# One attention unit for the 64-token tiles of two batches: one in each half of the 128 rows

## The chip, the cores and the metric

The kernel runs on one core of one Trainium2 chip. The metric is the device time of one execution, in microseconds (us). Times of instructions come from one profiled execution of the kernel.

## What is computed

Sliding-window attention with a linear bias by distance, then two feed-forward layers without a norm between them. Everything is float32.

```
B, H, S, D = 4, 8, 576, 64          # attention, window 128
scores = q @ k.T / 8 + slope[h] * -(i - j)      where 0 <= i - j < 128, else masked
attn   = softmax(scores);  x = attn @ v         -> 2304 tokens x 512
h = x @ w_in;   x = (h * sigmoid(h)) @ w_out     # 512 -> 2048 -> 512
h = relu(x @ w_in2);  out = (h * h) @ w_out2     # 512 -> 2048 -> 512
```

A batch has 576 tokens: four tiles of 128 and a last one of 64. Two heads make a pair; q and k come transposed, with the 64 numbers of the one head of a pair in rows 0 to 63 and those of the other in rows 64 to 127.

## The kernel before

**Blocks and units.** The 16 full tiles of the four batches make four blocks of 512 tokens, the four tiles of 64 tokens a fifth one of 256. A *unit* is one tile and one pair of heads: 64 full units (0 to 63), then 16 narrow ones (64 to 79), each of which fills rows 0 to 63 alone in the work by row.

**What is done for a unit.** `scores` (L247): TensorE, one matmul for each half of the query rows and each head, into one of two PSUM tiles, `so` (the first two of four units) or `pp` (the other two). `maxima` (L273, VectorE): bias and row minimum. `exponentials` (L283, ScalarE), `reciprocals` (L290, VectorE), `normalise` (L300, GpSimd). `transpose_p` (L331, TensorE, again into `so` and `pp`), `copy_p` (L344, or L347 and L348 for narrow units, ScalarE), `values` or, for narrow units, `values_of_four` (L380, L361, TensorE, into `o`), `x_hi` (L391, ScalarE) and `x_lo` (L395, VectorE): the block's x as the sum of two reduced floats.

**Slots.** From unit 20 on attention runs inside the loop of the first layer. A *slot* n (0 to 63, L1019) is one chunk of 128 columns of w_in for one block of 512 tokens: 12 matmuls of 128x512 in `mm1` (L564). All engines get their instructions in the order in which this loop writes them. Four units go together: scores of units u to u+3 in slot n = u - 20 ahead of its `mm1`; transposes in slot n+3; values in slot n+7 (n+6 where they are narrow):

```
for n in range(4, (NB - 1) * NF, 4):
    u = n0 + n
    narrow = u < NU and units[u][4] < P
    visits[n][2] = some(*range(u, u + 4))
    visits[n + 2 if narrow else n + 3][0] = some(*range(u - 4, u))
    visits[n + 3][1] = some(*range(u, u + 4))
```

Here [2] are scores, [1] transposes, [0] values. At the end of a slot come the loads: q and k of units u+4 to u+7 in the slot of the scores of u to u+3, v of the next four units in the slot of the values of four. Tiles "q", "k" and "v" have four buffers each. The last line of a slot is `store_t(n - 2)`.

**Queues.** Nearly all DMAs are issued by SyncE (SP), in order: an issue that waits holds all that stand behind it. `act1(n)` (L582, ScalarE) writes tanh(h/2) of slot n to one of four buffers, `ts[:, n % 4]`; `store_t(n)` (L592) sends it to DRAM (`g0d`), and `act1(n + 4)` waits for that store to land. ScalarE's order in a slot with values and transposes is `act1(n - 1)`, `x_hi`, `copy_p`; the next scores into `so` and `pp` wait for the copies out of them.

**Weights.** w_in and w_out are brought in as 64-bit words and converted, one tile of two chunks at a time, in five steps in slots that follow each other (`w_first`, `w_abs`, `w_join`, `w_hi`, `w_lo`); `begin` (L841) says in which slot a tile begins. The 16 buffers "w" hold the 16 converted tiles in the end; until then some serve as `spare` room.

After slot 63 come slots of the fifth block (L553), the second matmul (L631), and the second layer (L692, L785).

Of the kernel before, what the change touches and what calls it, by code (L numbers as in the profile page):

```python
# [8 lines left out]
F32 = mybir.dt.float32  # L9
# [7 lines left out]
P = 128  # L17
# [8 lines left out]
def kernel(  # L26
# [21 lines left out]
    nc = tc.nc  # L48
    B, NHP, S, _ = v.shape
    NT, DM = out.shape  # L50
    NF = w1.shape[0]
    D = 64
# [18 lines left out]
    full = [(b, t, P, min(t, P)) for b in range(B) for t in range(0, S - P + 1, P)]  # L71
    rest = [(b, S // P * P, S % P, P) for b in range(B)]
    blocks = [full[i:i + NSUB] for i in range(0, len(full), NSUB)]
    blocks.append(rest)
    NB = len(blocks)
    width = [sum(t[2] for t in tiles) for tiles in blocks]
    start = [sum(width[:j]) for j in range(NB)]
    assert sum(width) == NT and max(width) <= BLK and P % rest[0][2] == 0
    tbs = []
    for j, tiles in enumerate(blocks):  # L80
        c0 = 0
        for t in tiles:
            tbs.append((j, c0) + t)
            c0 += t[2]
    units = [t + (hp,) for t in tbs for hp in range(NHP)]
    NU = len(units)
    x_t = {}

# [6 lines left out]
    def attention(ap, ps, n0):  # L95
        slope = [2.0 ** (-8.0 * (h + 1) / H) for h in range(H)]
        xq, xk, xv, z_t, s_t, pt_t, o_t = ({} for _ in range(7))
        c = {"n0": n0}

        W = 3 * D

        def halves_of(u):

            n, m0 = units[u][4:6]
            if m0 == P:
                return [(slice(0, n), slice(0, W))]
            if u < c["n0"] and not m0:
                return [(slice(0, n), slice(D, W))]  # L110
            return [(slice(i * D, (i + 1) * D), slice(P - m0 - i * D, W)) for i in range(n // D)]

        def whole(u):

            n, m0 = units[u][4:6]
            return slice(0, n), slice(D + P - m0 - (n - D if m0 < P else 0), D + W)

        def zeros(z):
            nc.gpsimd.memset(z[..., :D], 0.0)
            nc.gpsimd.memset(z[..., D + W:], 0.0)  # L120

# [70 lines left out]
        def load_v_strip(i):  # L192
# [6 lines left out]
            for hp in range(NHP):  # L199
                xv[i * NHP + hp] = [c["va"][:, i - 1, hp] if m0 else None, c["va"][:, i, hp]]  # L200

        def load_qk(u):
            _, _, b, t0, n, m0, hp = units[u]
            if u not in xq:
                xq[u] = ap.tile([P, P], F32, tag="q", name="q", bufs=4)
                nc.sync.dma_start(out=xq[u][:, :n], in_=q[b, hp, :, t0:t0 + n])
            xk[u] = ap.tile([P, 2 * P], F32, tag="k", name="k", bufs=4)[:, P - m0:P + n]
            nc.sync.dma_start(out=xk[u], in_=k[b, hp, :, t0 - m0:t0 + n])

        def load_v(u):  # L210
            _, _, b, t0, n, m0, hp = units[u]
            t = ap.tile([P, 2, P], F32, tag="v", name="v", bufs=4)
            if m0 == n:
                nc.sync.dma_start(
                    out=t, in_=v[b, hp, t0 - m0:t0 + n, :].rearrange("(k p) d -> p k d", p=P)
                )
            else:
                if m0:
                    nc.sync.dma_start(out=t[:m0, 0], in_=v[b, hp, t0 - m0:t0, :])
                nc.sync.dma_start(out=t[:n, 1], in_=v[b, hp, t0:t0 + n, :])  # L220
            xv[u] = [t[:, 0], t[:, 1]]

        def scores(u):


            _, _, b, t0, n, m0, hp = units[u]
            lo = P - m0
            xq_, xk_ = xq.pop(u), xk.pop(u)
            apart = len(xq_.shape) == 3
            if apart:  # L230
                s = acc_p.tile([P, 2, 2 * P], F32, tag="acc", name="s")
                s = [s[:, j] for j in range(2)]
            else:
                so = c["pp" if u >= c["n0"] and u % 4 > 1 else "so"]
                s = [so[:, j, u % 2 * 2 * P:(u % 2 + 1) * 2 * P] for j in range(2)]
            if u < c["n0"] and not m0:
                for j in range(2):
                    nc.tensor.matmul(
                        s[j][:D, D:P], lhsT=c["far"], rhs=c["ident"][:, :D], start=True, stop=True
                    )  # L240
            for i in range(n // D):
                for j in range(2):
                    r = slice(i * D, (i + 1) * D)
                    first = max(lo - i * D, 0)
                    keys = slice(first + i * D - lo, W + i * D - lo)
                    h = slice(0, P) if apart else slice(j * D, (j + 1) * D)
                    nc.tensor.matmul(  # L247
                        s[j][r, first:W], lhsT=xq_[:, j, r] if apart else xq_[h, r], rhs=xk_[h, keys],
                        start=True, stop=True,
                    )  # L250
            s_t[u] = s
# [96 lines left out]
                copy(to[:n, :, 1::2], pp[:n, :, 1::2])  # L348
            pt_t[u] = pt

        def values_of_four(u):

            *_, n, m0, _ = units[u]
            pts, vts = [[t.pop(u + i) for i in range(4)] for t in (pt_t, xv)]
            o = c["o"]
            for i in range(4):
                o_t[u + i] = o[:, i - i % 2:i - i % 2 + 2]
            for kb, m in ((0, m0), (1, n)):
                for i in range(4):
                    for j in range(2):  # L360
                        nc.tensor.matmul(  # L361
                            o[j * D:(j + 1) * D, i, :n], lhsT=vts[i][kb][:m, j * D:(j + 1) * D],
                            rhs=pts[i][:m, j, kb, :n], start=kb == i == 0, stop=kb == 1,
                            skip_group_check=True,
                        )

        def values(u):
            _, _, b, t0, n, m0, hp = units[u]
            pt, vt = pt_t.pop(u), xv.pop(u)
            if u % 2 == 0:  # L370
                o = c["o"]
                if u < c["n0"] - 4 and u % 4:
                    o = c.pop("late", None) or acc_p.tile([P, 4, P], F32, tag="acc", name="o")
                first = u % 4 if u >= c["n0"] - 4 else 0
                o_t[u] = o[:, first:first + 2]
            o = o_t[u - u % 2][:, u % 2]
            for kb, m in ((0, m0), (1, n)):
                if m:
                    for j in range(2):
                        nc.tensor.matmul(  # L380
                            o[j * D:(j + 1) * D, :n], lhsT=vt[kb][:m, j * D:(j + 1) * D],
                            rhs=pt[:m, j, kb, :n], start=kb == 0 or not m0, stop=kb == 1,
                        )
# [9 lines left out]
        def x_lo(u):  # L393
            xh, xl, o = halves_of_x(u)
            nc.vector.tensor_tensor(xl, o, xh.bitcast(F32), ALU.subtract)  # L395

        return (zeros, lambda: c["z"], wake, constants, biases, load_q_apart, load_k_strip, load_v_strip, load_qk, load_v, scores, maxima, exponentials,
                reciprocals, normalise, transpose_p, copy_p, values, values_of_four, x_hi, x_lo)

# [2 lines left out]
    def spare(dtype):  # L404

        return wp.tile([P, 16 * P], F32R, tag="w", name="spare").bitcast(dtype)
# [123 lines left out]
    for b in range(NB):  # L530
        m = BLK // width[b]
        slots += [(b, tuple(range(f, f + m))) for f in range(0, NF, m)]
    NS = len(slots)
    NI = NF // 2
# [304 lines left out]
    begin = {}  # L839
    for i in range(NI):  # L840
        begin[0, 0, i] = 2 * i - 4  # L841
        begin[0, 1, i] = 2 * NI + 5 * i
    converted = [(0, 0, i) for i in range(EARLY + 1)]
    begin[0, 0, EARLY + 1] = 1

# [35 lines left out]
    with tc.manual_schedule():  # L881
        def ends(j):

            return sum(1 for u in units if u[0] <= j)

        n0 = ends(0) + 4
        with tc.tile_pool(name="at", bufs=2) as ap, tc.tile_pool(
            name="ps", bufs=1, space=bass.MemoryType.PSUM
        ) as ps:
            (zeros, at_z, wake, constants, biases, load_q_apart, load_k_strip, load_v_strip, load_qk, load_v, scores, maxima, exponentials,  # L890
             reciprocals, normalise, transpose_p, copy_p, values, values_of_four, x_hi, x_lo) = attention(ap, ps, n0)
            assert [t[1:4] for t in blocks[0]] == [(i * P, P, min(i, 1) * P) for i in range(NSUB)]
            load_k_strip(0, slice(0, 1))
            load_q_apart(0)
# [100 lines left out]
            def some(*us):  # L995
                return [u for u in us if u < NU]
# [4 lines left out]
            visits = {n: [(), (), ()] for n in range((NB - 1) * NF)}  # L1001
            for n in range(4, (NB - 1) * NF, 4):
                u = n0 + n
                narrow = u < NU and units[u][4] < P
                visits[n][2] = some(*range(u, u + 4))
                visits[n + 2 if narrow else n + 3][0] = some(*range(u - 4, u))
                visits[n + 3][1] = some(*range(u, u + 4))
            u = n0
            visits[1] = (), (u - 2, u - 1), ()
# [8 lines left out]
            left = []  # L1018
            for n in range((NB - 1) * NF):  # L1019
                old, mid, new = visits[n]  # L1020
                if len(old) == 4 and units[old[0]][4] < P:
                    values_of_four(old[0])
                else:
                    for u in old:
                        values(u)
                for u in mid:
                    transpose_p(u)
                for u in new:
# [51 lines left out]
        with tc.tile_pool(name="gp", bufs=1) as gp_, tc.tile_pool(  # L1080
            name="acc2", bufs=4, space=bass.MemoryType.PSUM
# [29 lines left out]
            for i in range(4):  # L1111
                n = 4 + 10 * i
# [9 lines left out]
            for j, x in enumerate(((1, 1, 3), (1, 1, 4))):  # L1122
                n = 18 + 10 * j
# [5 lines left out]
            for i in range(5, NI):  # L1129
                n = (29, 42, 57)[i - 5]  # L1130
# [23 lines left out]
            for s in range(1, 4):  # L1154
                c = 7 * 4 * s - 21
# [57 lines left out]
            for n in range(NS):  # L1213
# [6 lines left out]
                b, fs = slots[n]  # L1220
# [22 lines left out]
            for c in range(4 * NI // 2):  # L1243
                s = 2 * c // NI
# [105 lines left out]
```

## Time and profile before

| | us |
|---|---|
| runs of the kernel, median (lowest to highest) | 871.03 (869.74 to 871.57) |
| the profiled execution, its time | 870.38 |
| its span in the trace | 868.6 |
| TensorE busy in the span | 857.1 |
| slots 44 to 63, from the first scores of a narrow unit to the end of slot 63 | 209.38 to 283.83 of the span |

In the rows, PE is TensorE's matmuls and PEld its weight loads, DVE is VectorE, ACT ScalarE, POOL GpSimd, SPq the issues of SyncE. A float32 matmul of the program is two records of the trace, so 8 matmuls of attention are 16 records; those of `mm1` are one each.

### The profile page before, as it was taken

The page shows a single profiled execution, that of the slowest core. Times are in us where ns is not written, and L with a number is a line of the kernel's source. Part 1 is how long each engine was busy: PE and PEld are TensorE (multiplying, and loading weights), DVE is VectorE, ACT ScalarE, POOL GpSimd, SP SyncE. Part 2 cuts the span into 40 slices and gives each one's busy share as a digit, 9 for nine tenths or more (in the row PEclk, how much of TensorE's full clock was granted, in tenths as well). Part 3 has the DMA queues.
Part 4 walks back from the last instruction along what each step waited for, and adds up shares of the span by engine and source line. Part 5 has one row for each costly group of instructions (what it writes and reads, how often), then busy time and mean ns, then how long its engine had stood idle before and what let it go on. Part 6 is the DMA issues. An engine that isn't in the chain of part 4 may idle for free.

```text
span 868.6 us, 17368 instructions
## 1 busy us (share of the span) xinstructions
PE 857.1 (99%) x6344; PEld 763.4 (88%) x6344; DVE 595.2 (69%) x1290; ACT 460.5 (53%) x1010; POOL 137.1 (16%) x222
## 2 busy tenths in 40 slices
PE   7999999999999999999999999999999999999997
PEld 6778888787778888888888899999999999999997
DVE  6878665656552465998646546677467799989883
ACT  8778666666563443555333456556566743343331
POOL 6788333434431000000000000000000000000000
PEclk9999999999999999999999999999999999999999
DMA  9676766776542377799875454565457954444431
GB/s 265 196 220 220 209 187 188 216 224 193 153 147 97 117 256 248 261 345 355 278 275 193 145 179 160 197 248 194 160 201 300 348 178 148 135 147 129 138 108 39
DMA packets 114469, 173.64 MB, mean 200 GB/s; under 512 B 12240, under 2 KB 73680, under 8 KB 111824
## 3 DMA queue, kind: packets, MB, share of 16 engines
q1 hardware_dynamic: 114112, 172.40, 60.2%
q8 instruction: 50, 0.82, 0.4%
q14 instruction: 35, 0.29, 0.1%
q10 hardware_dynamic: 272, 0.13, 0.1%
HBM read 111.15 MB, written 61.34 MB: 199 GB/s over the span
## 4 chain that ended last, share of the span: by engine, by line
PE 94%; DMA 2%; SPq 1%; DVE 1%; ACT 1%; POOL 1%; issue 0%; DVEq 0%; ACTq 0%; POOLq 0%
PE acc L631 23%; PE acc L785 21%; PE h L564 19%; PE a L692 12%; PE d L692 6%; PE b L692 3%; PE o L380 3%; PE h L553 3%; PE so L247 1%; PE pp L331 1%; PE pp L247 1%; DMA g0d<-t 1%; PE so L331 1%; DMA spare<-in_w_dram 1%; PE o L361 1%; SPq L174 1%
## 5 line engine op out<-in xcount | busy, mean ns | idle before, releaser
L631 PE MATMUL acc<-g,w 128*128 128x512 f32 (+1 forms) x896 | 196.9, 382 | 0.0
L631 PEld LDWEIGHTS acc<-g,w 128*128 128x128 f32 x896 | 163.8, 188 | 32.9
L564 PE MATMUL h<-x,w 128*128 128x512 f32 x768 | 185.7, 396 | 0.0
L785 PE MATMUL acc<-w,g 128*128 128x256 f32 x1512 | 181.6, 283 | 0.0
L785 PEld LDWEIGHTS acc<-w,g 128*128 128x128 f32 x1512 | 181.5, 192 | 0.0
L564 PEld LDWEIGHTS h<-x,w 128*128 128x128 f32 x768 | 141.2, 188 | 34.6 <-DVE st L273 2.5
L692 PE MATMUL a<-x,w 128*128 128x288 f32 x720 | 104.0, 295 | 0.0
L692 PEld LDWEIGHTS a<-x,w 128*128 128x128 f32 x720 | 98.6, 188 | 0.2 <-DVE ev L823 0.2
L611 ACT CAST g<-l 128x512 fp32r<-128x512 f32 x72 | 44.8, 622 | 99.0 <-PE acc L631 84.8
L612 DVE TENSOR_TENSOR g<-l,g 128x512 fp32r<-128x512 f32 x72 | 49.7, 690 | 54.7 <-ACT g L611 54.3
L300 POOL TENSOR_SCALAR z<-z,st 128x192 f32<-128x192 f32 (+2 forms) x120 | 62.4, 537 | 108.0 <-DVE st L294 77.3
L587 DVE SCALAR_TENSOR_TENSOR t<-t,h 128x512 f32<-128x512 f32 x64 | 43.7, 683 | 47.9 <-ACT t L582 47.8
L582 ACT ACTIVATE t<-h 128x512 f32<-128x512 f32 x64 | 38.2, 596 | 53.3 <-PE h L564 45.4
L283 ACT ACTIVATE z<-z,st 128x192 f32<-128x192 f32 (+2 forms) x120 | 52.3, 438 | 14.8 <-DVE st L273 14.6
L759 ACT CAST g<-l 128x1024 fp32r<-128x1024 f32 x25 | 26.2, 1050 | 61.1 <-issue 30.8
L692 PE MATMUL d<-x,w 128*128 128x288 f32 x384 | 56.4, 295 | 0.0
L692 PEld LDWEIGHTS d<-x,w 128*128 128x128 f32 x384 | 52.9, 188 | 0.0
L273 DVE CUSTOM_DVE_ANT_0 z<-so,bias 128x192 f32<-128x192 f32 (+2 forms) x68 | 19.5, 328 | 30.2 <-PE so L247 26.5
L453 POOL TENSOR_TENSOR w<-spare,w 128x512 fp32r<-128x512 f32 x24 | 36.8, 1553 | 5.7 <-ACT w L448 5.6
L1272 DVE TENSOR_TENSOR ev<-a,ev 128x288 f32<-128x288 f32 x32 | 14.1, 454 | 32.7 <-PE a L692 32.0
L766 DVE TENSOR_TENSOR g<-l,g 128x1024 fp32r<-128x1024 f32 x25 | 30.6, 1224 | 8.2 <-ACT g L759 8.2
L523 DVE TENSOR_TENSOR w<-raw,w 128x1024 fp32r<-128x1024 f32 (+1 forms) x22 | 23.7, 1087 | 10.1 <-ACT w L518 10.1
(160 smaller groups left out, 1157.6 us busy)
## 6 DMA issues: line engine op xcount, KB each, us to landing
g0d<-t SPq DMA_DIRECT2D x72, 256.0 KB, 2.8
l<-g0d SPq DMA_DIRECT2D x72, 256.0 KB, 5.0
raw<-in_w_dram SPq DMA_DIRECT2D x28, 512.0 KB, 5.4
g1d<-t SPq DMA_DIRECT2D x48, 288.0 KB, 2.4
l<-g1d SPq DMA_DIRECT2D x50, 256.0 KB, 3.3
spare<-in_w_dram SPq DMA_DIRECT2D x12, 1024.0 KB, 8.0
wd<-raw SPq DMA_DIRECT2D x10, 1024.0 KB, 4.7
raw<-wd SPq DMA_DIRECT2D x7, 1024.0 KB, 5.7
```

The costliest lines, as they stand in the source:

```text
L283: nc.scalar.activation(z[r, j, k], z[r, j, k], AF.Exp, bias=least[r, j:j + 1], scale=-1.0, accum_out=total[r, j:j + 1],)
L300: nc.gpsimd.tensor_scalar(z[r, j, k], z[r, j, k], share[r, j:j + 1], 1.0, ALU.mult, ALU.mult)
L453: nc.gpsimd.tensor_tensor(w[:, 1, a], words(x)[1][:, a].bitcast(F32), w[:, 0, a].bitcast(F32), ALU.subtract)
L564: nc.tensor.matmul(h[:, j * w:(j + 1) * w], lhsT=wi[:, wh, c * P:(c + 1) * P], rhs=x[:, xh, c, :w], start=c == 0 and i == 0, stop=c == KC ...
L582: nc.scalar.activation(t_t[n], h_t[n], AF.Tanh, scale=0.5)
L587: nc.vector.scalar_tensor_tensor(t, t, 1.0, h, ALU.add, ALU.mult)
L611: nc.scalar.copy(g[:, 0], t)
L612: nc.vector.tensor_tensor(g[:, 1], t, g[:, 0].bitcast(F32), ALU.subtract)
L631: nc.tensor.matmul(to, lhsT=wo[:, a, c * P:(c + 1) * P], rhs=g[:, z, j * w:(j + 1) * w], start=f == 0 and i == 0, stop=f == NF - 1 and i = ...
L692: nc.tensor.matmul(acc[to], lhsT=w[wh][:, c * P:(c + 1) * P], rhs=o[:, xh, c], start=r in (0, 1, 3) and c == 0 and k == 0, stop=c == 1 and ...
L766: tt(g[1][:, :, :4], a, g[0][:, :, :4].bitcast(F32), ALU.subtract)
L785: nc.tensor.matmul(acc[to][:, half], lhsT=g[x][a], rhs=w[y][:, b], start=i == 0 and half == 0 and j == 0, stop=i == NI - 1 and j == 2, ski ...
```

## The change

The fifth block's units are made over: unit 64 to 71 instead of 64 to 79, each with the 64-token tiles of two batches, b and b+1, in rows 0 to 63 and 64 to 127. Such a *double* unit has the shapes of a full one in scores, maxima, exponentials, transposes and copies, and the rules for full units place it: scores in slots 44 and 48, transposes in 47 and 51, values in 51 and 55. For each it loads a q tile from two batches and two k tiles, one for each batch. The second k tile is taken from tag "v", which full units use for v. The v rows of two batches and all four pairs go to one shared tile `c["vs"]` (a "w" buffer, two corners set to zero by GpSimd), by four DMAs for four units. w_out tile 6 begins in slot 53 instead of 46, tile 7 in 56 instead of 51.

```diff
-    units = [t + (hp,) for t in tbs for hp in range(NHP)]
+    units = [t + (hp,) for t in tbs[:len(full)] for hp in range(NHP)]
+    twos = [t[:4] + (P, P) for t in tbs[len(full)::2]]
+    units += [t + (hp,) for t in twos for hp in range(NHP)]
...
+        def load_double_qk(u):
+            _, _, b, t0, _, _, hp = units[u]
+            xq[u] = ap.tile([P, P], F32, tag="q", name="q", bufs=4)
+            nc.sync.dma_start(
+                out=xq[u].rearrange("p (b c) -> p b c", b=2),
+                in_=q[b:b + 2, hp, :, t0:t0 + D].rearrange("b p c -> p b c"),
+            )
+            xk[u] = [
+                ap.tile([P, 2 * P], F32, tag=tag, name=tag, bufs=4)[:, :W] for tag in "kv"
+            ]
+            for i, to in enumerate(xk[u]):
+                nc.sync.dma_start(out=to, in_=k[b + i, hp, :, t0 - P:t0 + D])
+
+        def load_double_v(u):
+
+            _, _, b, t0, _, _, hp = units[u]
+            if hp == 0:
+                if "vs" not in c:
+                    c["vs"] = spare(F32).rearrange("p (h i k d) -> p i k h d", h=NHP, i=2, k=2)
+                    nc.gpsimd.memset(c["vs"][D:, 0, 1], 0.0)
+                    nc.gpsimd.memset(c["vs"][:D, 1, 0], 0.0)
+                for i, kb, r, t in (
+                    (0, 0, slice(0, P), t0 - P), (0, 1, slice(0, D), t0),
+                    (1, 0, slice(D, P), t0 - P), (1, 1, slice(0, P), t0 - D),
+                ):
+                    nc.sync.dma_start(
+                        out=c["vs"][r, i, kb],
+                        in_=v[b + i, :, t:t + r.stop - r.start, :].rearrange("h p d -> p h d"),
+                    )
+            xv[u] = c["vs"][:, :, :, hp]
...
-        def values_of_four(u):
...
+        def values_of_double(u, o):
+            pt, vt = pt_t.pop(u), xv.pop(u)
+            for kb in range(2):
+                for i in range(2):
+                    for j in range(2):
+                        h, r = (slice(x * D, (x + 1) * D) for x in (j, i))
+                        nc.tensor.matmul(
+                            o[h, r], lhsT=vt[:, i, kb, h], rhs=pt[:, j, kb, r],
+                            start=kb == i == 0, stop=kb == 1, skip_group_check=True,
+                        )
...
-        begin[0, 1, i] = 2 * NI + 5 * i
+        begin[0, 1, i] = 2 * NI + 5 * i + (i == 6) * 7 + (i == 7) * 5
...
-                narrow = u < NU and units[u][4] < P
-                visits[n + 2 if narrow else n + 3][0] = some(*range(u - 4, u))
+                visits[n + 3][0] = some(*range(u - 4, u))
```

The order of the instructions on TensorE, first before, from the scores of units 68 to 71 (slot 48) to the transposes of the same units (slot 51; of these 16 rows the first two stand here):

```order
L247 MATMUL so<-k,q 64x192 x4
L247 MATMUL pp<-k,q 64x192 x4
L564 MATMUL h<-x,w 128x512 x24
L361 MATMUL o<-pt,v 64x64 x16
L564 MATMUL h<-x,w 128x512 x12
L331 MATMUL so<-ident,z 128x64
L331 MATMUL so<-ident,z 64x64
```

And of the changed kernel, from the scores' last row in slot 48 to slot 64 (its line 604 is the old line 564, its line 400 is `values_of_double`):

```order
L290 MATMUL pp<-v,q 64x192 x2
L604 MATMUL h<-x,w 128x512 x36
L400 MATMUL o<-pt,spare 64x64 x32
L374 MATMUL so<-ident,z 128x64 x16
L374 MATMUL pp<-ident,z 128x64 x16
L604 MATMUL h<-x,w 128x512 x48
L400 MATMUL o<-pt,spare 64x64 x32
L604 MATMUL h<-x,w 128x512 x108
```

Values and transposes now stand beside each other in one slot, there are two groups of four units instead of four, and nine slots of `mm1` follow without attention.

The second place is SyncE's queue at the end of slot 40, where q and k of units 64 to 67 are loaded; the word "waits" lists what an issue waits for (DMAHW: an earlier DMA, PE: a matmul). Before:

```order
L208 DMA k<-in_k_dram 128x192 [waits DMAHW2_49]
L206 DMA q<-in_q_dram 128x64 [waits DMAHW3_49,PE_49]
L208 DMA k<-in_k_dram 128x192 [waits DMAHW4_49]
L206 DMA q<-in_q_dram 128x64 [waits DMAHW5_49,PE_49]
L208 DMA k<-in_k_dram 128x192 [waits DMAHW6_49]
L206 DMA q<-in_q_dram 128x64 [waits DMAHW7_49,PE_49]
L208 DMA k<-in_k_dram 128x192 [waits DMAHW0_49]
L592 DMA g0d<-t 128x512 [waits DMAHW1_49,DVE_49]
```

In the changed kernel, from the k tile of the first batch of unit 64 to the same store (line 632):

```order
L220 DMA k<-in_k_dram 128x192 [waits DMAHW2_49]
L220 DMA v<-in_k_dram 128x192 [waits DMAHW4_49,DMAHW3_49,PE_49]
L212 DMA q<-in_q_dram 128x2x64
L220 DMA k<-in_k_dram 128x192 [waits DMAHW5_49]
L220 DMA v<-in_k_dram 128x192 [waits DMAHW6_49,PE_49]
L212 DMA q<-in_q_dram 128x2x64 [waits DMAHW7_49]
L220 DMA k<-in_k_dram 128x192 [waits DMAHW0_49]
L220 DMA v<-in_k_dram 128x192 [waits DMAHW1_49,PE_49]
L212 DMA q<-in_q_dram 128x2x64 [waits DMAHW2_49]
L220 DMA k<-in_k_dram 128x192 [waits DMAHW3_49]
L220 DMA v<-in_k_dram 128x192 [waits DMAHW4_49,PE_49]
L632 DMA g0d<-t 128x512 [waits DMAHW5_49,DVE_49]
```

Four loads into tiles "v" have come in. Each takes the buffer of the v tile of a full unit (56 for the first one), and the matmul that it waits for is the last one of that unit's values, in slot 43. The store in the last row is `store_t(38)`. The same order stands at the end of slot 44, for units 68 to 71, the values of units 60 to 63 (slot 47), and `store_t(42)`.

## Rows read from the trace of the kernel before

**Rows 1.** The page, part 1: busy time of the engines.
```profile
PE 857.1 (99%) x6344; PEld 763.4 (88%) x6344; DVE 595.2 (69%) x1290; ACT 460.5 (53%) x1010; POOL 137.1 (16%) x222
```
**Rows 2.** Stretches: us, busy us of five engines (instructions), granted clock, DMA share, GB/s.
```profile
209.38:283.83 74.45, 74.45 (x529) 58.39 (x529) 33.84 (x116) 39.13 (x131) 22.18 (x38) 1.00 0.45 144
...
864.10:868.60 4.50, 0.00 (x0) 0.00 (x0) 1.33 (x3) 0.00 (x0) 0.00 (x0) 1.00 0.31 117
```
**Rows 3.** Timeline of TensorE, four full units: start, us, line, operation, records.
```profile
187.53 1.97 PE L380 MATMUL o<-pt,v 128*64 128x128 f32 x32
189.43 0.71 PE L331 MATMUL so<-ident,z 64*128 64x64 f32 x16
...
190.57 3.01 PE L564 MATMUL h<-x,w 128*128 128x512 f32 x12
193.51 0.88 PE L247 MATMUL so<-k,q 64*64 64x192 f32 x16
194.21 0.83 PE L247 MATMUL pp<-k,q 64*64 64x192 f32 x16
194.97 8.49 PE L564 MATMUL h<-x,w 128*128 128x512 f32 x36
```
**Rows 4.** Timeline of TensorE, narrow units, slots 50 to 54 and 58 to 63.
```profile
232.56 1.30 PE L361 MATMUL o<-pt,v 128*64 128x64 f32 x32
233.79 3.04 PE L564 MATMUL h<-x,w 128*128 128x512 f32 x12
236.76 0.68 PE L331 MATMUL so<-ident,z 64*128 64x64 f32 x8
...
237.84 3.03 PE L564 MATMUL h<-x,w 128*128 128x512 f32 x12
240.80 0.87 PE L247 MATMUL so<-k,q 64*64 64x192 f32 x8
...
242.24 5.78 PE L564 MATMUL h<-x,w 128*128 128x512 f32 x24
247.95 1.30 PE L361 MATMUL o<-pt,v 128*64 128x64 f32 x32
...
268.61 11.19 PE L564 MATMUL h<-x,w 128*128 128x512 f32 x48
279.73 1.30 PE L361 MATMUL o<-pt,v 128*64 128x64 f32 x32
```
**Rows 5.** Timeline of all engines, slots 31 and 32; brackets: idle before, what ended it.
```profile
160.95 0.60 ACT L582 ACTIVATE t<-h 128x512 f32<-128x512 f32 x1 [4.13 <-DMA g0d<-t]
...
161.96 0.68 ACT L348 COPY pt<-so 128x256 f32<-128x256 f32 x2
...
162.69 0.88 PE L247 MATMUL so<-k,q 64*64 64x192 f32 x16
```
**Rows 6.** Timeline of all engines, slot 43.
```profile
204.10 1.92 SPq L214 DMA_DIRECT2D v<-in_v_dram  x4
204.87 0.58 ACT L582 ACTIVATE t<-h 128x512 f32<-128x512 f32 x1
...
206.13 1.08 ACT L344 COPY pt<-so 128x512 f32<-128x512 f32 x2
...
207.09 1.10 ACT L344 COPY pt<-pp 128x512 f32<-128x512 f32 x2
```
**Rows 7.** Timeline, issues of q and k: one in slot 40, first and last of eight in slot 48.
```profile
196.42 1.48 SPq L208 DMA_DIRECT2D k<-in_k_dram  x1
...
225.99 0.33 SPq L206 DMA_DIRECT2D q<-in_q_dram  x1
...
229.24 0.42 SPq L208 DMA_DIRECT2D k<-in_k_dram  x1
```
**Rows 8.** DMA issues in 160 to 217 and 216 to 290: median us to landing.
```profile
g0d<-t SPq DMA_DIRECT2D x15, 256.0 KB, 3.3
...
g0d<-t SPq DMA_DIRECT2D x21, 256.0 KB, 2.2
```

More of the change, by code (lines that the diff above doesn't have):

```diff
@@ L84 @@
             c0 += t[2]
-    units = [t + (hp,) for t in tbs for hp in range(NHP)]
+    units = [t + (hp,) for t in tbs[:len(full)] for hp in range(NHP)]
+    twos = [t[:4] + (P, P) for t in tbs[len(full)::2]]
+    assert rest[0][2] == P // 2 and len(rest) % 2 == 0
+    units += [t + (hp,) for t in twos for hp in range(NHP)]
     NU = len(units)
@@ L102, in attention, with double @@
         W = 3 * D
+        def double(u):
+            return units[u][0] == NB - 1
         def halves_of(u):
@@ L200, in load_v_strip @@
                 xv[i * NHP + hp] = [c["va"][:, i - 1, hp] if m0 else None, c["va"][:, i, hp]]
+        def load_double_qk(u):
[26 more added lines that the diff above has]
+            xv[u] = c["vs"][:, :, :, hp]
         def load_qk(u):
+            if double(u):
+                return load_double_qk(u)
             _, _, b, t0, n, m0, hp = units[u]
@@ L210, in load_v @@
         def load_v(u):
+            if double(u):
+                return load_double_v(u)
             _, _, b, t0, n, m0, hp = units[u]
@@ L229, in scores @@
             apart = len(xq_.shape) == 3
+            if not double(u):
+                xk_ = [xk_[..., max(i * D - lo, 0):W + i * D - lo] for i in range(n // D)]
             if apart:
@@ L244, in scores @@
                     first = max(lo - i * D, 0)
-                    keys = slice(first + i * D - lo, W + i * D - lo)
                     h = slice(0, P) if apart else slice(j * D, (j + 1) * D)
                     nc.tensor.matmul(
-                        s[j][r, first:W], lhsT=xq_[:, j, r] if apart else xq_[h, r], rhs=xk_[h, keys],
+                        s[j][r, first:W], lhsT=xq_[:, j, r] if apart else xq_[h, r], rhs=xk_[i][h],
                         start=True, stop=True,
@@ L349, in copy_p @@
             pt_t[u] = pt
-        def values_of_four(u):
[L353 to L359, printed above, removed]
+        def values_of_double(u, o):
+            pt, vt = pt_t.pop(u), xv.pop(u)
+            for kb in range(2):
+                for i in range(2):
                     for j in range(2):
+                        h, r = (slice(x * D, (x + 1) * D) for x in (j, i))
                         nc.tensor.matmul(
-                            o[j * D:(j + 1) * D, i, :n], lhsT=vts[i][kb][:m, j * D:(j + 1) * D],
-                            rhs=pts[i][:m, j, kb, :n], start=kb == i == 0, stop=kb == 1,
-                            skip_group_check=True,
+                            o[h, r], lhsT=vt[:, i, kb, h], rhs=pt[:, j, kb, r],
+                            start=kb == i == 0, stop=kb == 1, skip_group_check=True,
                         )
@@ L368, in values @@
             _, _, b, t0, n, m0, hp = units[u]
-            pt, vt = pt_t.pop(u), xv.pop(u)
             if u % 2 == 0:
@@ L376, in values @@
             o = o_t[u - u % 2][:, u % 2]
+            if double(u):
+                return values_of_double(u, o)
+            pt, vt = pt_t.pop(u), xv.pop(u)
             for kb, m in ((0, m0), (1, n)):
@@ L397, in attention @@
         return (zeros, lambda: c["z"], wake, constants, biases, load_q_apart, load_k_strip, load_v_strip, load_qk, load_v, scores, maxima, exponentials,
-                reciprocals, normalise, transpose_p, copy_p, values, values_of_four, x_hi, x_lo)
+                reciprocals, normalise, transpose_p, copy_p, values, x_hi, x_lo)
     w_t, raw_t = {}, {}
@@ L890 @@
             (zeros, at_z, wake, constants, biases, load_q_apart, load_k_strip, load_v_strip, load_qk, load_v, scores, maxima, exponentials,
-             reciprocals, normalise, transpose_p, copy_p, values, values_of_four, x_hi, x_lo) = attention(ap, ps, n0)
+             reciprocals, normalise, transpose_p, copy_p, values, x_hi, x_lo) = attention(ap, ps, n0)
             assert [t[1:4] for t in blocks[0]] == [(i * P, P, min(i, 1) * P) for i in range(NSUB)]
@@ L1020 @@
                 old, mid, new = visits[n]
[L1021 to L1025, printed above, removed]
+                for u in old:
+                    values(u)
                 for u in mid:
```

## The prediction

> **What bounds the kernel now.** I read the page's busy times first: TensorE works 857.1 us, 99% of the span, VectorE 69%, ScalarE 53%, GpSimd 16% [rows 1]. A kernel so full gets shorter only by less work on TensorE, and longer by a wait that TensorE has not had. Next the table of stretches. From the first scores of a narrow unit to the end of slot 63, 74.45 us, which holds all that the change touches, TensorE is busy 74.45 of 74.45 us, at a granted clock of 1.00, the upper level (2.4 GHz); ScalarE is busy for 39, VectorE for 34 and GpSimd for 22 us [rows 2]. So the other engines' instructions that vanish there save nothing. What a piece of attention costs is read from TensorE's timeline, once where four full units are worked on [rows 3] and once where four narrow ones are [rows 4]: always from the start of a piece to the start of the next, since the durations in a row overlap. Last come the timelines of all engines and the landing of the stores [rows 5 to 8], for the new waits.
>
> **Less work on TensorE.** Sixteen narrow units are four groups of four; the eight double ones are two, and a double unit has the shapes of a full one.
>
> Scores: a narrow group takes 242.24 - 240.80 = 1.44 us [rows 4], a full one, with twice the records, 194.97 - 193.51 = 1.46 [rows 3]. Four of the one for two of the other: 5.76 to 2.92, a gain of 2.84. The matmuls of the two row halves evidently run beside each other in a full unit. A double unit's k and q also come in the two halves of a full one's shape, so I take the full price.
>
> Transposes: 237.84 - 236.76 = 1.08 a narrow group, 190.57 - 189.43 = 1.14 a full one: 4.32 to 2.28, a gain of 2.04.
>
> Values: 233.79 - 232.56 = 1.23 for a narrow group's 32 records, 4.92 in all. A double group has 64 records (32 matmuls), 64 columns each. No such group stands in the trace. The bound above is two narrow ones, 2.46; below it is a full group's values, 1.90, which stream as many columns in longer matmuls. I take 2.1, somewhat nearer the lower end, since the halves of the output rows can run side by side: 4.92 to 4.2, a gain of 0.7 (0 to 1.1).
>
> Fewer cuts of the first layer's stream: 12 matmuls between pieces of attention take 236.76 - 233.79 = 2.97 us, 24 take 247.95 - 242.24 = 5.71, 48 take 279.73 - 268.61 = 11.12 [rows 4]. From 24 to 48 that is 2.70 for each 12, so by about 2.72 for 12 matmuls each uninterrupted piece costs a further 0.25. Slots 44 to 63 are cut into 13 pieces before and 5 after (slots 44 to 46, 47, 48 to 50, 51 to 54, 55 to 63). Eight fewer: a gain of 2.0.
>
> Together 2.84 + 2.04 + 0.7 + 2.0 = 7.6 us (6.9 to 8.0).
>
> **What costs nothing.** Two memsets on GpSimd stand in slot 47 under 22 us of work in 74 [rows 2]; uncovered they would be some tenths. The four v loads of a double group have at least four slots, over 10 us, until the values, where a 256 KB store lands in 2.2 to 3.3 [rows 8]. w_out tiles 6 and 7 are converted in slots 53 to 60, whose VectorE, ScalarE and GpSimd have lost the work of narrow units, and they are first read in the second matmul; without that cover TensorE would wait at its start for the last step of a tile, which I take as 0.
>
> **The new wait.** A double unit's second k tile lies in a buffer of tag "v". At the end of slot 40 the first such load therefore waits for the values of unit 56 in slot 43. SP's queue is in order, so behind it stand nine more loads, then `store_t(38)`, and later `store_t(39)` and `store_t(40)`. Today the stores leave in their slots. `act1(42)` overwrites the buffer that `store_t(38)` reads, so ScalarE stops at it, with `x_hi` and the copies out of so and pp of slot 43 queued behind; and the scores of units 64 to 67 in slot 44 wait for these copies. The trace has this very chain on a smaller scale: `act1` stood idle for 4.13 us for a g0d store, its copies out of so ended at 161.96 + 0.68 = 162.64, and the scores began at 162.69 [rows 5]. The place in time:
>
> - The v tiles of slot 43 come free as today, when the v loads of that slot are issued: 204.10 [rows 6]. Then the first second-k load leaves.
> - `store_t(38)` is ten issues on. Eight such issues stood 3.25 us apart from first to last (225.99 to 229.24), 0.464 each [rows 7]: 204.10 + 4.64 = 208.74.
> - Landing: 3.3 us in the one half of the stage, 2.2 in the other [rows 8]; I take the middle, 2.75: 211.49.
> - From the start of `act1` to the end of the copies out of so: 206.13 + 1.08 - 204.87 = 2.34 [rows 6]: 213.83, and the scores at +0.05: 213.88.
> - They begin at 209.38 today [rows 2]: 4.50 us of idle TensorE.
> - The copies out of pp end 207.09 + 1.10 - 206.13 - 1.08 = 0.98 after those out of so [rows 6]; the scores into so take only 194.21 - 193.51 = 0.70 [rows 3]: 0.28 more.
>
> That is 4.78 us. At the end of slot 44 all of it stands a second time: units 68 to 71, the values of slot 47, `store_t(42)`, `act1(46)`, the scores of slot 48. Between the two, the v loads of units 60 to 63 wait for the first double scores, but the store behind them, `store_t(41)`, is wanted only two slots later. The values of slots 51 and 55 read other buffers, so there is no third stall. Two make 9.56 us. Low end: landing 2.2, no 0.28 at pp, thus about 4.0; I use 4.2, since three stores then share the queues. High end: landing 3.3 and one issue that is held as k was at 196.42, for 1.48 in place of 0.42 [rows 7]: 4.78 + 0.55 + 1.06 = 6.4.
>
> **The sum.** 2 x 4.78 - 7.6 = +2.0 us; between 2 x 4.2 - 8.0 = +0.4 and 2 x 6.4 - 6.9 = +5.9. The profiled execution took 870.38 us, 1.8 beyond its span of 868.6, and so would take 872.3; the runs' median lies 0.65 above it: 873.0 us, and 871.4 to 876.9 by the bounds.
>
> **The rivals.**
>
> *The stores don't hold TensorE, or hardly* (faster). The gain of 7.6 stands and the time is 863.4. It decides for "faster" where a stall is below (7.6 - 1.74) / 2 = 2.9 us, 1.74 us being 0.2% of the time, about what a measurement of this kernel tells from no change. For it speaks that most stores land long before their `act1`; against it that ten issues of 0.46 us alone, from 204.10 on, end beyond the 207.09 at which the last copies begin today. To get under 2.9 the store must land about 1.9 us earlier than I have it. Chance 0.10.
>
> *The two cancel* (within 0.2%). Each stall is between 2.9 and 4.67 us, of which 4.2 to 4.67 is inside my own bounds: about 871. Nothing but a landing of 2.2 to 2.6 is needed. Chance 0.22.
>
> *The clock falls in a stall* (slower by more). TensorE would pass 4.8 us without a matmul, twice, and restart at 1.2 GHz. In the rows the granted clock is still 1.00 over the 4.50 us after the last matmul [rows 2], and no idle of that length lies within the stream, so it is not shown which clock work after one gets. If one slot's 12 matmuls run at half rate, a fall costs another 2.72 us (an estimate): 875.7 with one, 878.4 with two. Chance 0.25. The Trainium skill (TensorE: Matmul & The Clock Gate, "Part 1: The HAM clock gate") says that the throttled clock is the default state, released by activity and back after idleness; by it one fall at least is likely here, and the trace of before, with the clock at 1.00 to its end, does not show it.
>
> *Double scores don't overlap as full ones do*, because a unit's two k tiles are separate ones. The gain of 2.84 is gone and it takes 875.8. The tiles have the same shapes and halves, so this is a small part, 0.05, of the forecast's upper side.
>
> The forecast itself, two stalls of 4.67 to 6.4 us at full clock, gets the other 0.38.
>
> **Range and chances.** Faster 0.10, same 0.22, slower 0.25 + 0.05 + 0.38 = 0.68. 870.5 to 878.0 leaves out the first rival, the bottom of the second, and two falls of the clock: just under 2 in 10. The forecast's own range is 872.7 to 876.9.
>
> **What the changed profile would show.** The first SP issue of k into a "v" tile waiting for TensorE's values, twice, and ScalarE's `act1` idle for over 6 us for a g0d store in slots 43 and 47. TensorE idle for 4.2 to 6.4 us ahead of the scores of slots 44 and 48, released by ScalarE's copies, and nowhere else in the stage. Scores at 1.46, transposes at 1.14, values near 2.1, and 36, 12, 36, 48 and 108 matmuls of the first layer in a row. The stage as a whole near 74.45 + 2.0 = 76.4, and after slot 63 the same times as before. The prediction is wrong if those idle stretches are short or missing (863), if the clock after them is below 1.00, or if TensorE waits at the second matmul for w_out.

## The result: 875.38 us, slower

The changed kernel takes 875.38 us (median of 6 runs, 874.09 to 877.04), the kernel before in the same and the earlier runs 870.01 (median of 6, 869.60 to 871.57): a ratio of 1.006, 95% interval 1.0049 to 1.0071, slower by 5.4 us. The forecast was 873.0, with 870.5 to 878.0 as its range: side and range hold, and the two stalls are the ones foretold. But the loss is over twice what the likeliest case said, since TensorE's clock fell at both stalls, and the range was drawn to leave out two such falls. The mean granted clock was 0.993 to 0.995 in all six executions; it is 0.999 or 1.000 in all 23 of the kernel before that were timed beside the later experiments.

**Profile after.** The profiled execution took 874.92 us. First TensorE's timeline from the transposes of slot 47 on, the pieces that answer to [rows 3, 4].

```profile
227.38 3.01 PE L604 MATMUL h<-x,w 128*128 128x512 f32 x12
234.75 0.58 PE L290 MATMUL so<-k,q 64*64 64x192 f32 x2 [4.35 <-ACT pt L387]
...
237.52 9.82 PE L604 MATMUL h<-x,w 128*128 128x512 f32 x36
247.26 2.09 PE L400 MATMUL o<-pt,spare 128*64 128x64 f32 x64
249.28 0.71 PE L374 MATMUL so<-ident,z 64*128 64x64 f32 x16
...
250.43 11.17 PE L604 MATMUL h<-x,w 128*128 128x512 f32 x48
...
263.55 24.78 PE L604 MATMUL h<-x,w 128*128 128x512 f32 x108
```

Values of a double group take 249.28 - 247.26 = 2.02 us (forecast 2.1) and transposes 1.15 (1.14); 36, 48 and 108 matmuls of the first layer follow each other as foretold. What doesn't fit are the scores, 237.52 - 234.75 = 2.77 in place of 1.46, and the 36 matmuls behind them, 9.82 by their row, where 36 such have 8.49 in [rows 3].

The chain of the wait, all engines in slots 43 and 44, answers to [rows 6, 7].

```profile
203.42 0.34 SPq L220 DMA_DIRECT2D v<-in_k_dram  x1
...
207.76 0.38 SPq L220 DMA_DIRECT2D v<-in_k_dram  x1
208.24 1.34 SPq L632 DMA_DIRECT2D g0d<-t  x3
210.69 0.60 ACT L622 ACTIVATE t<-h 128x512 f32<-128x512 f32 x1 [6.38 <-DMA g0d<-t]
...
211.70 1.10 ACT L387 COPY pt<-so 128x512 f32<-128x512 f32 x2
212.66 1.13 ACT L387 COPY pt<-pp 128x512 f32<-128x512 f32 x2
212.86 0.38 PE L290 MATMUL so<-k,q 64*64 64x192 f32 x2 [4.09 <-ACT pt L387]
```

Before, the same three stores left in slot 41 (the prediction had each leave in its own slot):

```profile
198.94 1.35 SPq L592 DMA_DIRECT2D g0d<-t  x3
```

Read the rows of the changed kernel downward: the first load of k into a v buffer leaves once slot 43's values have read that buffer, nine loads follow, and the three stores leave at 208.24, at the end of slot 43. ScalarE has waited 6.38 us for the first of them to land; then come `act1(42)`, x, the copies, and at last the scores.

The table of stretches: length, busy us of five engines (instructions), granted clock, DMA share, GB/s. From the end of slot 43's matmuls to slot 51 (without slot 47), and on to the end of slot 63 and of the last matmul.

```profile
208.72:212.86 4.14, 0.05 (x1) 0.00 (x1) 1.54 (x4) 2.17 (x6) 0.00 (x0) 1.00 0.64 224
212.86:215.35 2.49, 2.49 (x32) 1.49 (x33) 1.97 (x8) 2.05 (x6) 0.00 (x0) 0.57 0.18 54
215.35:217.00 1.65, 1.65 (x9) 1.38 (x6) 1.65 (x10) 1.65 (x9) 0.00 (x0) 0.62 0.59 161
217.00:224.33 7.33, 7.33 (x33) 5.77 (x31) 2.21 (x8) 3.56 (x10) 4.90 (x10) 1.00 0.24 77
230.35:234.75 4.40, 0.05 (x2) 0.00 (x1) 1.35 (x3) 2.17 (x6) 0.00 (x0) 0.88 0.95 277
234.75:237.52 2.77, 2.77 (x33) 1.79 (x33) 1.01 (x7) 2.03 (x6) 0.00 (x0) 0.50 1.02 302
237.52:240.60 3.08, 3.08 (x11) 2.47 (x8) 2.15 (x13) 2.14 (x10) 0.41 (x2) 0.51 0.59 182
240.60:247.26 6.66, 6.66 (x30) 5.25 (x28) 1.72 (x4) 2.07 (x6) 2.86 (x8) 1.00 0.52 186
247.26:288.16 40.90, 40.90 (x317) 34.29 (x317) 17.29 (x23) 15.40 (x25) 6.25 (x4) 1.00 0.40 132
288.16:868.60 580.44, 580.35 (x3881) 543.98 (x3879) 416.79 (x685) 273.44 (x458) 0.00 (x0) 1.00 0.59 204
```

TensorE idles twice, 4.14 and 4.40 us, and each time it works at half clock (0.50, 1.2 GHz) for some microseconds afterwards. That is where scores and matmuls lose their time. The stage that took 74.45 us [rows 2] runs from 208.72 to 288.16 here, 79.44: 5.0 us more. Behind it nothing differs: 580.44 us to the last matmul, against 864.10 - 283.83 = 580.27 before [rows 2].

### The profile page after: what moved, and what is told of

Its sections match the earlier page's. It is cut to its first block, busy times and chain, and to the rows that moved or that the text cites. A ratio compares the mean times of both kernels' runs of the same rounds, so it can differ in the third digit from the quotient of the medians.

```text
span 873.1 us, 17162 instructions
## 1 busy us (share of the span) xinstructions
PE 854.0 (98%) x6344; PEld 762.5 (87%) x6344; DVE 590.3 (68%) x1246; ACT 452.0 (52%) x950; POOL 131.6 (15%) x208
## 4 chain that ended last, share of the span: by engine, by line
PE 94%; SPq 2%; DMA 1%; ACT 1%; POOL 1%; issue 1%; DVE 1%; DVEq 0%; ACTq 0%; POOLq 0%
PE acc L671 23%; PE acc L825 21%; PE h L604 20%; PE a L732 12%; PE d L732 6%; PE b L732 3%; PE o L420 3%; PE h L593 3%; PE so L290 1%; PE pp L290 1%; PE pp L374 1%; DMA spare<-in_w_dram 1%; PE so L374 1%; DMA g0d<-t 1%; SPq L181 1%
## 5 line engine op out<-in xcount | busy, mean ns | idle before, releaser
L604 PEld LDWEIGHTS h<-x,w 128*128 128x128 f32 x768 | 143.3, 190 | 34.5 <-DVE st L316 2.5
L343 POOL TENSOR_SCALAR z<-z,st 128x192 f32<-128x192 f32 (+1 forms) x104 | 54.6, 544 | 102.1 <-DVE st L337 71.4
L326 ACT ACTIVATE z<-z,st 128x192 f32<-128x192 f32 (+1 forms) x104 | 45.3, 439 | 13.0 <-DVE st L316 12.8
L316 DVE CUSTOM_DVE_ANT_0 z<-so,bias 128x192 f32<-128x192 f32 (+2 forms) x60 | 17.1, 327 | 22.6 <-PE so L290 18.4
```

The source lines that it names most:

```text
L326: nc.scalar.activation(z[r, j, k], z[r, j, k], AF.Exp, bias=least[r, j:j + 1], scale=-1.0, accum_out=total[r, j:j + 1],)
L343: nc.gpsimd.tensor_scalar(z[r, j, k], z[r, j, k], share[r, j:j + 1], 1.0, ALU.mult, ALU.mult)
L604: nc.tensor.matmul(h[:, j * w:(j + 1) * w], lhsT=wi[:, wh, c * P:(c + 1) * P], rhs=x[:, xh, c, :w], start=c == 0 and i == 0, stop=c == KC ...
```

## The experiments

Each kernel was timed beside the kernel before, whose median was 870.29 us for the first four and 870.10 for the others.

**Second k tiles in a buffer of their own.** With the second tile of each unit in a weight buffer there is nothing to wait for.

```diff
-            xk[u] = [
-                ap.tile([P, 2 * P], F32, tag=tag, name=tag, bufs=4)[:, :W] for tag in "kv"
-            ]
+            if "ks" not in c:
+                c["ks"] = spare(F32)
+            xk[u] = [
+                ap.tile([P, 2 * P], F32, tag="k", name="k", bufs=4)[:, :W],
+                c["ks"][:, (u - 64) * W:(u - 63) * W],
+            ]
```

> The changed kernel, with the second k tiles in a weight buffer of their own in place of the buffers of tag v; as many loads of the same size. Theory (the loads wait for the values of slots 43 and 47 and hold the stores behind them, and the clock falls in the two idle stretches that follow): neither idle stretch is there, the clock stays at 1.00, and the time is 875.4 - 8.5 (4.14 and 4.40 us of idle) - 4.2 (slower scores and first-layer matmuls after them) = 862.7, between 861.5 and 864. Rival 1 (it is the four more loads, their traffic or their issue time, that make the stores late, not the wait): some 4 us of idle stay ahead of the scores, 873 to 876. Rival 2 (the double units themselves save less than the sum of 7.6 us): 864 to 868.

Measured: 863.31 us, ratio 0.9915 (0.9901 to 0.9928). SP, `act1(42)` and TensorE around slot 43, and the stage from there to the end of slot 63:

```profile
203.54 1.34 SPq L635 DMA_DIRECT2D g0d<-t  x3
207.23 0.59 ACT L625 ACTIVATE t<-h 128x512 f32<-128x512 f32 x1
...
211.73 0.38 PE L293 MATMUL so<-k,q 64*64 64x192 f32 x2
...
213.19 8.49 PE L607 MATMUL h<-x,w 128*128 128x512 f32 x36
```

```profile
211.73:278.35 66.62, 66.62 (x529) 54.88 (x529) 28.48 (x72) 30.36 (x71) 16.38 (x24) 1.00 0.48 153
```

The three stores leave at 203.54, ahead of slot 43, and `act1(42)` has no idle time before it now (6.38 us in the changed kernel). The scores take 213.19 - 211.73 = 1.46 us, and TensorE is busy for all of the 66.62 us. As many loads as in the changed kernel don't hurt (rival 1), and the double units save 74.45 - 66.62 = 7.83 us of the stage, what the sum had as 7.6 (rival 2).

By the medians of the runs the kernel is 7.0 us faster than the kernel before, 0.8 less than by the stage. The profiled execution, 866.13 us, is the longest of the five, and its trace shows a loss outside the stage, among the first units:

```profile
19.01:22.08 3.07, 0.00 (x1) 0.04 (x1) 2.62 (x7) 1.26 (x2) 0.00 (x0) 0.93 1.03 406
22.08:25.02 2.94, 2.94 (x24) 2.33 (x24) 2.69 (x13) 1.34 (x5) 1.85 (x4) 0.50 0.73 222
```

TensorE idles for 3.07 us there, and the clock stands at 0.50 over the work that follows; in the kernel before the idle stretch at this place is 1.75 us long, and the clock stays at 1.00. The two executions with a mean clock of 1.000 took 862.07 and 862.08 us, 8.2 less than the kernel before.

**The store ahead of the loads.** The wait stays; what stands behind it changes. The edit moves the store in every slot.

```diff
+                store_t(n - 2)
                 for u in new:
                     if u + 4 < NU:
                         load_qk(u + 4)
...
-                store_t(n - 2)
```

> The changed kernel, with the store of a slot written ahead of its loads of q and k: the wait for the v buffers stays as it is, but the stores that the tanh of slots 42 and 46 wait for no longer stand behind it. Theory (it is what stands behind the wait, not the wait or the late loads): both idle stretches go but for some tenths, since the last k and q tiles, issued near 207.8, land about when their scores begin; the clock stays at 1.00: 862.5 to 864.5. Rival (the loads that wait come too late themselves): idle stretches of over 2 us stay, released by a DMA of q or k, 867 to 875.

Measured: 863.30 us, ratio 0.9923 (0.9910 to 0.9937), inside the theory's span. SP, ScalarE and TensorE in slots 43 and 44, and the stage:

```profile
203.21 0.34 SPq L220 DMA_DIRECT2D v<-in_k_dram  x1
204.01 0.57 ACT L622 ACTIVATE t<-h 128x512 f32<-128x512 f32 x1
...
208.03 1.36 SPq L632 DMA_DIRECT2D g0d<-t  x3
208.49 0.38 PE L290 MATMUL so<-k,q 64*64 64x192 f32 x2
...
210.22 5.97 PE L604 MATMUL h<-x,w 128*128 128x512 f32 x25
210.42 0.60 ACT L622 ACTIVATE t<-h 128x512 f32<-128x512 f32 x1 [3.15 <-DMA g0d<-t]
```

```profile
208.49:275.76 67.27, 67.27 (x529) 55.08 (x529) 28.73 (x72) 30.06 (x71) 16.36 (x24) 1.00 0.55 173
```

The second k loads still leave only once slot 43's values have read their buffers, and three stores still leave behind them, at 208.03. But `store_t(38)` is no longer among them, it left at 189.67: `act1(42)` does not wait, and the 3.15 us that the next `act1` waits hold up nothing that TensorE needs. The late loads cost some tenths: the scores take 210.22 - 208.49 = 1.73 us, and 1.86 in slot 48, in place of 1.46, and the stage is 0.65 us longer than with a buffer more. So nearly all of the loss lies with the stores that were shut in, not with the loads.

**The waiting loads last.** q and the first k of four units, then the four second ones.

```diff
-            for i, to in enumerate(xk[u]):
-                nc.sync.dma_start(out=to, in_=k[b + i, hp, :, t0 - P:t0 + D])
+            nc.sync.dma_start(out=xk[u][0], in_=k[b, hp, :, t0 - P:t0 + D])
+            if hp == NHP - 1:
+                for j in range(NHP):
+                    nc.sync.dma_start(out=xk[u - hp + j][1], in_=k[b + 1, j, :, t0 - P:t0 + D])
```

> The changed kernel, with the loads in another order: q and the first k tiles of all four units, then the four second ones, which wait. Only four issues in place of ten then stand between the end of the wait and the store. Theory (the size of the idle stretch is the number of issues at 0.46 each, and then the landing of the store): the store leaves at about 205.3 and lands at 207.7, the scores begin 1.2 us late in place of 4.1, twice, and the clock does not fall: 875.4 - 6.2 - 4.2 = 865.0, between 864 and 866.5. Rival (the landing of the store or the copies set the stretch, the issues ahead of it don't): over 870.

Measured: 866.12 us, ratio 0.9948 (0.9936 to 0.9961). SP, ScalarE and TensorE in slots 43 and 44:

```profile
206.14 1.36 SPq L634 DMA_DIRECT2D g0d<-t  x3
208.63 0.60 ACT L624 ACTIVATE t<-h 128x512 f32<-128x512 f32 x1 [3.46 <-DMA g0d<-t]
210.80 0.38 PE L292 MATMUL so<-k,q 64*64 64x192 f32 x2 [1.16 <-ACT pt L389]
...
212.59 3.69 PE L606 MATMUL h<-x,w 128*128 128x512 f32 x15
```

The store stands four issues behind the wait, `act1` waits 3.46 in place of 6.38 us and TensorE 1.16 in place of 4.09 (1.19 the second time): 2.9 us less for six issues, 0.49 each. The clock stays at 1.00, so the smaller wait, the one at pp, can be seen: the scores take 212.59 - 210.80 = 1.79 us, 0.33 more than without a stall, since the copies out of pp end later than the scores into so. The prediction has it as 0.28.

**More work in the idle stretches.** This tests the clock by itself: first-layer matmuls of slots 43 and 47 issued again.

```diff
                 mm1(n)
+                if n in (43, 47):
+                    mm1(n)
```

> The changed kernel with more work: the 12 first-layer matmuls of slots 43 and 47 are issued twice (the second time into another buffer, with the same numbers), so that TensorE works 2.7 us of each idle stretch. Theory (the clock falls because TensorE idles for over 4 us): the idle left is 1.4 and 1.7 us, the clock stays at 1.00, the scores after it take 1.46 us and not 2.5 and 2.8, and the kernel with 5.4 us more work is faster by about 4.2: 871.2, between 870.3 and 872. Rival (the double scores are slow for another cause: their two k tiles, or the loads that run beside them): 875 to 876, and scores of 2.5 us.

Measured: 873.69 us, ratio 1.0042 (1.0029 to 1.0055): faster than the changed kernel, as expected, but not to 871.2. Stretches around slot 44, then slot 48:

```profile
211.55:212.96 1.41, 0.01 (x2) 0.01 (x1) 1.41 (x4) 1.41 (x5) 0.00 (x0) 1.00 0.06 20
212.96:214.75 1.79, 1.69 (x33) 1.03 (x33) 1.65 (x6) 1.73 (x4) 0.00 (x0) 1.00 0.03 10
```

```profile
231.91:234.55 2.64, 0.00 (x1) 0.00 (x0) 1.35 (x3) 2.17 (x6) 0.00 (x0) 1.00 0.99 271
234.55:235.00 0.45, 0.45 (x12) 0.43 (x16) 0.00 (x0) 0.45 (x2) 0.00 (x0) 1.00 0.89 236
235.00:237.02 2.02, 2.02 (x28) 0.88 (x20) 1.24 (x9) 1.82 (x6) 0.00 (x0) 0.54 1.01 264
```

The first stretch is 1.41 us long now and the clock stays at 1.00. The second is 2.64, longer than the 1.7 that I had expected, since one of the q loads ahead of the store took 1.65 us to issue in place of 0.43 (why is not shown), and `act1(46)` waited longer; and there the clock falls, half a microsecond after the scores have begun. This left it open whether the idle stretch or something else in slots 47 and 48 lowers the clock, so one more kernel filled the second stretch further.

```diff
-            for c in range(KC):
+            for last in {43: [KC], 47: [2, KC]}.get(n, []) + [KC]:
+                for c in range(last):
...
-                        start=c == 0 and i == 0, stop=c == KC - 1 and i == 2,
+                            start=c == 0 and i == 0, stop=c == last - 1 and i == 2,
```

> The changed kernel, with first-layer matmuls issued again into the same buffer, 12 more in slot 43 and 18 more in slot 47, so that of the two idle stretches 1.4 and about 1.3 us are left (with 12 more in each, 1.40 and 2.64 us were left, and the clock fell after the second alone). Theory (a long idle stretch is what lowers the clock, and nothing else in these slots does): the clock stays at 1.00 from slot 43 to 51, the scores take 1.46 to 1.8 us, and the time is 875.4 - 4.2 = 871.2, between 870.3 and 872.2. Rival (something else in slot 47, the loads that land beside the scores, say, slows them and the matmuls): the second half-speed stretch stays, and 873 to 875.

Measured: 872.16 us, ratio 1.0026 (1.0015 to 1.0036). Each idle stretch with the scores and 36 matmuls behind it:

```profile
211.16:212.65 1.49, 0.01 (x2) 0.01 (x1) 1.49 (x4) 1.49 (x5) 0.00 (x0) 1.00 0.05 19
212.65:222.82 10.17, 10.07 (x68) 7.70 (x68) 5.83 (x24) 7.13 (x22) 4.61 (x10) 1.00 0.33 95
232.96:233.81 0.85, 0.01 (x1) 0.00 (x0) 0.68 (x3) 0.85 (x3) 0.00 (x0) 1.00 1.13 339
233.81:243.99 10.18, 10.08 (x69) 7.71 (x69) 4.88 (x23) 6.25 (x21) 3.27 (x8) 1.00 0.76 249
```

With the second stretch at 0.85 us the clock stays at 1.00 in slot 48 too, beside as much DMA traffic (339 and 249 GB/s; the changed kernel had 277 in its second stretch). So what lowers it is the idle stretch, or goes with it: a kernel with 30 matmuls (6.8 us) more work is 3.2 us faster than the changed one. The same pieces, scores and 36 matmuls, took 224.33 - 212.86 = 11.47 and 247.26 - 234.75 = 12.51 us in the changed kernel: the falls cost 1.30 and 2.33 us here. The time is still 1 us over what I had expected, for two reasons that the rows show: at full clock the 0.33 us at pp come out, twice, and a q load took 1.29 us to issue in slot 47's queue, so that the scores of slot 48 began 4.97 us after the first 12 matmuls of slot 47 (233.81 - 225.87 - 2.97) in place of 4.40.

**The wait alone, in the kernel before.** The narrow k tiles of units 64 to 67 take the v buffers; nothing else is changed.

```diff
-            xk[u] = ap.tile([P, 2 * P], F32, tag="k", name="k", bufs=4)[:, P - m0:P + n]
+            tag = "v" if 64 <= u < 68 else "k"
+            xk[u] = ap.tile([P, 2 * P], F32, tag=tag, name=tag, bufs=4)[:, P - m0:P + n]
```

> The kernel before, with the wait alone: the k tiles of units 64 to 67 take buffers of tag v, as the second k tiles of the change do; nothing else is moved. Theory (the wait and what stands behind it are enough, with no double units): the store of slot 38 leaves seven issues after the values of slot 43, at about 206.7, and lands 2.4 us later; TensorE idles for some 2.5 us ahead of the scores of slot 44, once: 870.3 + 2.5 = 872.8, and up to 874.5 if the clock falls. Rival (the idle stretches need the double units, by their loads or their copies): 870 to 871.

Measured: 873.35 us, ratio 1.0044 (1.0031 to 1.0056). In the profiled execution, slots 43 and 44:

```profile
206.93 1.35 SPq L593 DMA_DIRECT2D g0d<-t  x3
209.30 0.60 ACT L583 ACTIVATE t<-h 128x512 f32<-128x512 f32 x1 [4.76 <-DMA g0d<-t]
211.47 0.87 PE L248 MATMUL so<-v,q 64*64 64x192 f32 x8 [2.46 <-ACT pt L345]
```

```profile
208.97:211.47 2.50, 0.04 (x2) 0.01 (x1) 1.54 (x4) 2.17 (x6) 0.00 (x0) 1.00 0.44 169
211.47:213.24 1.77, 1.66 (x16) 0.94 (x16) 1.67 (x6) 1.75 (x4) 0.00 (x0) 0.99 0.03 10
213.24:216.00 2.76, 2.76 (x9) 2.18 (x8) 2.42 (x15) 2.76 (x13) 0.11 (x1) 0.50 0.70 184
```

The store leaves at 206.93 and TensorE idles for 2.50 us, as worked out, with no double unit in the program. The clock falls here too, 1.8 us after the work has begun again. This execution took 875.28 us. Its mean granted clock is 0.997. Of the other four, two have 0.995 and 0.997 (875.25 and 873.35 us) and two 0.999 (873.06 and 872.42 us): so after this wait the clock does not seem to fall, or not as far, every time. Where it fell in those four no trace shows.

**Fewer cuts alone, in the kernel before.** Narrow units are placed by the rules for full ones: 9 pieces in place of 13.

```diff
-                visits[n + 2 if narrow else n + 3][0] = some(*range(u - 4, u))
+                visits[n + 3][0] = some(*range(u - 4, u))
```

> The kernel before, with one edit: narrow units are placed as full ones, so that their transposes and values stand in one slot, and slots 44 to 63 are cut into 9 pieces in place of 13. Theory (each uninterrupted piece of the first layer costs 0.25 us beyond its matmuls): 4 pieces fewer, 870.3 - 1.0 = 869.3, between 868.8 and 869.8. Rival (the 0.25 belongs to the switch to attention and not to the cut, or the copies come late behind x_hi): 870 or more.

Measured: 869.40 us, ratio 0.9991 (0.9982 to 0.9999). The times barely tell it from nothing, but the trace shows it: from the first scores of slot 44 to the end of slot 63 the stage takes 73.48 us in place of 74.45.

```profile
208.72:282.20 73.48, 73.48 (x530) 58.72 (x529) 35.68 (x116) 39.17 (x131) 22.14 (x38) 1.00 0.44 146
```

That is 0.24 us for each of the 4 cuts, so the 0.25 stands.

**The later w_out tiles alone, in the kernel before.**

```diff
-        begin[0, 1, i] = 2 * NI + 5 * i
+        begin[0, 1, i] = 2 * NI + 5 * i + (i == 6) * 7 + (i == 7) * 5
```

> The kernel before, with the later conversion of w_out tiles 6 and 7 alone (slots 53 and 56 in place of 46 and 51). Theory (their steps lie under TensorE's work in either place, and nothing waits for them at the second matmul): 870.3, within 0.5. Rival (they are last before the second matmul, and TensorE waits there for the last step): 871 to 874.

Measured: 870.11 us, ratio 0.9999 (0.9989 to 1.0008). That part of the change costs and brings nothing.

## Why the prediction held, and where it did not

The account of the stage, each part from a row: idle TensorE 4.14 + 4.40 = 8.54; the wait at pp 2 x 0.33 = 0.66; half clock 1.30 + 2.33 = 3.63; saved 7.83 (from the kernel with no wait). Together +5.0 us, and the stage is 79.44 - 74.45 = 4.99 longer. (The 0.33 is from the kernel with the waiting loads last, where the clock stays up; half clock is what the same pieces took beyond the kernel with the stretches filled.)

- **Less work, 7.6 us: right.** 7.83 measured, with scores of 1.46, transposes of 1.15, values of 2.02 and five pieces of the first layer in slots 44 to 63. By the run medians it is 7.0.
- **What costs nothing: right**, by the profile behind slot 63, by the run of the w_out part alone, and by the stage of 66.62 us in which TensorE waits for neither the memsets nor the v loads.
- **The wait, 9.56 us: right in place, chain and size.** 8.54 + 0.66 = 9.20. Step by step for the first stall: from the first v buffer to the store 208.24 - 203.42 = 4.82 (forecast 4.64), landing 210.69 - 208.24 = 2.45 (2.75), from `act1` to the scores 2.17 (2.39). The kernel with a buffer more is rid of the whole of it, the one with the store ahead of all but 0.65 us; with the store ten, four and seven issues behind the start of the wait, TensorE idled for 4.1, 1.2 and 2.5 us.
- **"Two stalls at full clock" as the likeliest case: wrong.** This is the step that failed: the sum counts every piece behind a stall at 1.00 and puts the fall of the clock at nothing. The runs showed half clock behind both stalls, 1.30 + 2.33 = 3.63 us, and so the prediction's own sign of being wrong, a clock below 1.00 after the idle stretches, was there. At full clock the parts give 9.20 - 7.83 = +1.4 us. That is under the 1.74 us which the prediction called "the two cancel" (chance 0.22): 9.20 / 2 = 4.60 us a stall, where "slower" needed 4.67. So it was the clock that made the kernel clearly slower, and not the wait alone.
- **The case that came** was the third rival with both falls, at 878.4 and a chance of 0.25 for one or two. Its price was too high: 2.72 us for a fall, where 1.30 and 2.33 were measured, in part since the slow scores hide the wait at pp. Its chance was too low. I leaned on a clock of 1.00 over the 4.50 us behind the last matmul [rows 2]; that row holds no matmul after the idle time, and so says nothing of the clock that the next one gets. The profile now shows this clearly: in the stretch of 4.14 us the clock also stands at 1.00, and 0.57 in the one behind it.
- **That the time lies in the range is luck.** The range was drawn to leave out two falls. Two came, and 875.38 is inside because they cost 1.8 us less than 2 x 2.72, the wait was 0.4 shorter and the gain 0.2 larger than in the sum, and the base was 1.0 too high: the sum starts from 871.03, the median of three runs, where six gave 870.01. From there the same sum gives 872.0.

The Trainium skill (TensorE: Matmul & The Clock Gate, "Part 1: The HAM clock gate") has the throttled clock as the state that idleness brings back. The trace agrees: 0.50 to 0.62 behind idle stretches of 4.14 and 4.40 us, and 1.00 in slots 44 and 48 where these were taken away, or filled until 1.49 us or less was left.

## What to carry to other kernels

A buffer that is "free by then" isn't free where an in-order DMA queue reaches the load three slots early: count what stands behind the load, above all stores whose source someone wants to write again. Here the order of two lines, or a buffer elsewhere, turned 0.6% slower into 0.8% faster (863.3 against 875.4 us), with the same work. Where a bound TensorE gets an idle stretch of some microseconds, price the half clock after it as well as the stretch.

## What was not expected of the hardware

The clock falls late. It fell during the idle time in the stretches of 4.40 us (0.88 over it) and, among the first units of the kernel with a buffer more, 3.07 us (0.93); after 4.14, 2.64 and 2.50 us of idle it stood at 1.00 when the matmuls began again, and fell with TensorE already at work: 0.45 us later after 2.64, 1.8 after 2.50, and some 0.4 after 4.14 (an estimate from 0.57 over the first 2.49 us of work). After idle stretches of 0.85, 1.16, 1.19, 1.41 and 1.49 us in these slots, and of 1.75 us among the first units of the kernel before, it did not fall. So a short idle stretch can cost more than its own length, and the row of the stretch itself doesn't show it: the rows behind it do. Whether the length of the stretch alone decides is not shown.
